# Float32 weights in place for both layers of experts 0 to 4, high and low parts in both layers of experts 5 to 7

## The chip, the cores and the metric

The kernel runs on one core of a Trainium2 chip. The metric is the device time of one execution in microseconds (us), the median of several runs. The profiles show one profiled execution each; their times are counted from the first instruction.

## The reference, cut to what matters

```python
def _moe2_ref(x, w_gate, w1, w2):            # N, D = 2304, 512; E = 8 experts; F = 1024
    N, D = x.shape
    E = w_gate.shape[1]
    cap = N // E                              # 288 tokens for each expert
    logits = x @ w_gate
    order = np.argsort(-logits.flatten())     # best (token, expert) pairs first
    ...                                       # a pair is taken if its token is free
    ...                                       # and its expert has under cap tokens
    out = np.zeros((N, D), dtype=np.float32)
    for e in range(E):
        mask = assigned == e
        h = np.maximum(x[mask] @ w1[e], 0.0)
        out[mask] = h @ w2[e]
    return out.astype(np.float32)

def reference(**kwargs):
    attn_out = _attn_ref(...)                 # 4 x 8 heads, 576 positions, causal, decayed
    x = attn_out.transpose(0, 2, 1, 3).reshape(2304, 512)
    x = _moe_ref(x=x, ...)                    # relu(x @ w_in)**2 @ w_out, 512 -> 2048 -> 512
    return _moe2_ref(x=x, ...)                # the part that the change touches
```

All inputs and the output are float32.

## The kernel before, in words

The kernel has three parts that overlap in time: attention, the first feed-forward layer (`moe1_chunk`), and the routed experts (`phase` and `expert`). The change touches only the last, which runs from about 685 us to the end.

**Routing.** `phase(m)` is called for m = 0 to 7. Each call finds the expert that fills up next, in what order is a matter of the data, and the 288 tokens that belong to it. It is one long chain of small VectorE (DVE) instructions with trips to TensorE (PE) between them: three rounds, each of which builds one-hot matrices on DVE (L1009, L1012), counts with 18 small matmuls (L1023), sums with two more (L1028, L1038), and shifts and masks on DVE (L1034, L1037, L1039, L997 and following). The last phase has no rounds. The result is the expert's number `ei` and the token list `idx`. Phase m+1 can't begin before phase m has its result. "Expert m" below is the one that phase m finds.

**Experts.** `expert(m, idx, widx)` reads the expert's number into a register of SyncE (SP), which issues the weight loads: four transfers of 512 KB for each of the two layers (for m = 0 the first layer has eight of 256 KB). GpSimd (POOL) gathers the 288 token rows by three indirect transfers (`xg`, L1151). TensorE transposes them (L1218), and the two layers follow: `up(f)` for eight blocks of 128 hidden features (L1234 to L1236, four steps k each, 32 groups in all) and, for each of four output blocks d, eight steps f (L1259, 32 in all). The result is copied (`ys`), transposed back (L1275), copied (`yo`) and written out by three indirect transfers of POOL (L1282).

**Two ways to multiply.** In *high and low parts* a matrix is split in two float32r matrices: the high part is a rounded copy (ScalarE, ACT, L381 from `rnd`), the low part is the difference (POOL, L1190; DVE may do it for m = 0 alone). A product is then three matmuls: high by high, low by high, high by low. A weight chunk lands in a raw buffer `wr` (four of them) and takes one slot for the high and one for the low part. In *plain float32* a chunk lands in its slot by the DMA itself, nothing is split, and a product is one matmul instruction, which the trace shows as two records. Before the change the first layer is in parts for all eight experts; the second is plain for m = 0 to 6 (`PLAIN = range(E - 1)`) and in parts for m = 7.

**Slots.** The weights lie in 32 slots named `z`, 16 for the first layers and 16 for the second (`us`). High parts take only the eight even ones of their 16, low parts only the odd ones; a plain chunk takes any of the 16, the even ones first.

**What sets the order.** Every operation is a task with a cost for each engine that could do it (`s.op({"pe": ...})`) and a priority (`s.base`). `Sched.run` simulates these costs once, when the kernel is built, and picks for each engine the ready task of the highest priority; `Sched.emit` writes the instructions in that order. So each engine works through a fixed list, and waits if the next instruction of its list isn't ready, whatever stands behind it. Routing has priority over the gather, and the gather over the rest of an expert (`20 + m`, `28.5 + m`, `30 + m`). The simulated costs know nothing of one engine slowing another.

Of the kernel before, what the change touches and what calls it, by code (L numbers as in the profile page):

```python
# [8 lines left out]
F = mybir.dt.float32  # L9
R = mybir.dt.float32r  # L10
# [11 lines left out]
CAP = NT // E  # L22
# [14 lines left out]
HV = [0]  # L37
# [3 lines left out]
UT = [("pt", 0), ("sc", 0), ("sc", 1)]  # L41
NH = 8

PLAIN = range(E - 1)
NX = 1
NWR = 4
YA = [("acc", 0), ("acc", 1)]
# [4 lines left out]
WG = 0  # L52
# [266 lines left out]
def dve1(n):  # L319
    return 70 + 1.04 * n  # L320
# [6 lines left out]
def act(n, psum=False, extra=0):  # L327
    return (51 if psum else 93) + 0.833 * n + 93 * extra
# [38 lines left out]
class K:  # L367
# [774 lines left out]
    def expert(self, m, idx, widx):  # L1142
        s, nc, ep = self.s, self.nc, self.ep
        IO = bass.IndirectOffsetOnAxis
        whi, wlo = [[], []], [[], []]
        plain = m in PLAIN
        xg = s.buf(ep, [96, 3, DM], F, "xg", 1)

        def gather_x():
# [11 lines left out]
        def wload(which, i):  # L1161

            src = (self.w1, self.w2)[which].rearrange("e p f -> p e f")
            us = [t for t in range(16) if (t % 4 >= 2) == which]
            if which and plain:
                wt = s.buf(self.wp, [128, 1024], F, "w1p", 0, also=[("z", 2 * t + x) for x in range(2) for t in us])
                whi[which].append(wt)

                def load(c0, c1, hold=False, after=None):
                    s.op({"sp": 450.0}, lambda e: e.dma_start(  # L1170
                        out=wt.t, in_=src[:, bass.ds(ev["v"], 1), 1024 * i:1024 * i + 1024].rearrange("p e f -> p (e f)")),
                        r=[widx] + ([(xg, WG)] if hold else []), w=[wt], nbytes=128 * 4096, after=after)
                return load
            raw = s.buf(ep, [128, 1024], F, "wr", NWR) if m else s.buf(self.wp, [128, 1024], F, "wr0", 0, also=self.zs(12, 13))
            hi = s.buf(self.wp, [128, 1024], R, f"w{which}h", 0, also=[("z", 2 * t) for t in us])
            lo = s.buf(self.wp, [128, 1024], R, f"w{which}l", 0, also=[("z", 2 * t + 1) for t in us])
            whi[which].append(hi)
            wlo[which].append(lo)
            halves = m == 0 and which in HV
            pr = P0 if m == 0 else None  # L1180

            def load(c0, c1, hold=False, after=None):
                key = c0 if halves else None
                s.op({"sp": 450.0}, lambda e: e.dma_start(
                    out=raw[:, 512 * c0:512 * c1], in_=src[:, bass.ds(ev["v"], 1), 1024 * i + 512 * c0:1024 * i + 512 * c1].rearrange("p e f -> p (e f)")),
                    r=[widx] + ([(xg, WG)] if hold else []), w=[(raw, key)], nbytes=128 * 2048 * (c1 - c0), after=after)
                for c in range(c0, c1):
                    cs = slice(512 * c, 512 * c + 512)
                    s.op(hi_alts(512, "act"), lambda e, cs=cs: self.rnd(e, hi[:, cs], raw[:, cs]), r=[(raw, key)], w=[(hi, c)], prio=pr)
                    s.op(lo_alts(512, LOE(m, which, i, 0, c)), lambda e, cs=cs: e.tensor_sub(lo[:, cs], raw[:, cs], hi[:, cs].bitcast(F)), r=[(raw, key), (hi, c)], w=[(lo, c)], prio=pr)  # L1190
            return load
# [23 lines left out]
        for k in range(4):  # L1215
            pt = s.buf(self.ps, [128, 512], F, "xt", 0, also=XT + (XA if m == 0 else []))
            for g in range(3):
                s.op({"pe": 107.0}, lambda e, k=k, g=g, pt=pt: e.transpose(pt[:, 96 * g:96 * g + 96], xg[:, g, k * 128:k * 128 + 128], self.ident[:96, :96]),  # L1218
                     r=[(xg, g), self.ident], w=[pt])
            h = s.buf(ep, [128, CAP], R, f"exh{k}", NX)  # L1220
            l = s.buf(ep, [128, CAP], R, f"exl{k}", NX)
            s.op({"act": act(CAP, True)}, lambda e, h=h, pt=pt: e.activation(h.t, pt[:, :CAP], AF.Copy), r=[pt], w=[h])
            s.op({"dve": dve1(CAP)}, lambda e, h=h, l=l, pt=pt: e.tensor_sub(l.t, pt[:, :CAP], h.t.bitcast(F)), r=[pt, h], w=[l])
            xh.append(h)
            xl.append(l)
        s.base = 30 + m

        def up(f):
            fs = slice(f * 128, f * 128 + 128)
            c = f // 4  # L1230
            u = s.buf(self.ps, [128, 512], F, "u", 2, also=UT)
            for k in range(4):
                def g(e, k=k):
                    e.matmul(u[:, :CAP], whi[0][k][:, fs], xh[k].t, start=(k == 0), stop=False)  # L1234
                    e.matmul(u[:, :CAP], wlo[0][k][:, fs], xh[k].t, start=False, stop=False)  # L1235
                    e.matmul(u[:, :CAP], whi[0][k][:, fs], xl[k].t, start=False, stop=(k == 3))  # L1236
                s.op({"pe": mm(CAP, 3)}, g, r=[(whi[0][k], c), (wlo[0][k], c), xh[k], xl[k]], w=[u])
            if plain:
                hh = s.buf(ep, [128, CAP], F, "ehh", NH)
                s.op({"act": act(CAP, True), "dve": dve1(CAP)}, lambda e: e.activation(hh.t, u[:, :CAP], AF.Relu) if e is nc.scalar else  # L1240
                     e.tensor_scalar(hh.t, u[:, :CAP], 0.0, None, op0=OP.max), r=[u], w=[hh])
                return hh, None
            hh = s.buf(ep, [128, CAP], R, "ehh", NH)
            s.op({"act": act(CAP, True)}, lambda e: e.activation(hh.t, u[:, :CAP], AF.Relu), r=[u], w=[hh])
            hl = s.buf(ep, [128, CAP], R, "ehl", NH)
            s.op({"dve": dve1(CAP)}, lambda e: e.scalar_tensor_tensor(hl.t, u[:, :CAP], 0.0, hh.t.bitcast(F), op0=OP.max, op1=OP.subtract), r=[u, hh], w=[hl])
            return hh, hl
# [3 lines left out]
        for d in range(4):  # L1251
            acc = s.buf(self.ps, [128, 512], F, "y", 0, also=YA)
            for f in range(8):
                def g(e, f=f, acc=acc, d=d):
                    hh, hl = hs[f]
                    wh = whi[1][f // 2]
                    ds = slice(512 * (f % 2) + d * 128, 512 * (f % 2) + d * 128 + 128)
                    if plain:
                        e.matmul(acc[:, :CAP], wh[:, ds], hh.t, start=(f == 0), stop=(f == 7))  # L1259
                        return  # L1260
                    wl = wlo[1][f // 2]
                    e.matmul(acc[:, :CAP], wh[:, ds], hh.t, start=(f == 0), stop=False)  # L1262
                    e.matmul(acc[:, :CAP], wl[:, ds], hh.t, start=False, stop=False)  # L1263
                    e.matmul(acc[:, :CAP], wh[:, ds], hl.t, start=False, stop=(f == 7))  # L1264
                if plain:
                    s.op({"pe": 1.89 * CAP}, g, r=[hs[f][0], whi[1][f // 2]], w=[acc])
                    continue
                s.op({"pe": mm(CAP, 3)}, g, r=[*hs[f], (whi[1][f // 2], f % 2), (wlo[1][f // 2], f % 2)], w=[acc])
            ys = s.buf(ep, [128, CAP], F, "ys", 2)
# [124 lines left out]
```

## Time and profile before

| | |
|---|---|
| median of 3 runs | 1049.22 us (1048.82 to 1049.54) |
| the profiled execution's own time | 1047.0 us |
| its span, first to last instruction | 1044.9 us |
| mean granted TensorE clock | 0.957 of full speed |
| PE busy | 951.6 us (91% of the span) |
| DVE busy | 646.0 us (62%) |
| ACT busy | 413.4 us (40%) |
| POOL busy | 359.6 us (34%) |
| splits of weights on POOL in the expert stage, in groups of 128x512 | 64 from `wr`, 81.3 us |

PE is the busiest engine over the whole span, but the share is an average. The 40 slices of the page show it at 5 to 9 tenths in the last third, where the granted clock falls below full speed several times too. The profiled execution's time is 2.1 us above its span, and 2.2 us below the median of the runs.

### The profile page before, as it was taken

Reading aid. Unit: us, or ns where it says so; the run is one execution under the profiler, and the core shown is the slowest. Engines: PE = TensorE matmul, PEld = TensorE weight load, DVE = VectorE, ACT = ScalarE, POOL = GpSimd, SP = SyncE. Lnnn points to the kernel's source line nnn. Section 1 sums busy time; section 2 is a strip of 40 time slices with the busy share of each in tenths; the row PEclk is TensorE's granted clock in tenths of the full one; section 3 lists DMA queues with packets and bytes.
Section 4 is the critical chain, followed back from the end, with each engine's and each line's share of the span. In section 5 each row is a group of like instructions: output and inputs, shape, how many; then the busy total and the mean of one; then the engine's idle time right before and its main releaser. Section 6 shows DMA issues by size and latency. Waiting matters only on the chain. (4 is left out here: it accounts for less than half of the span.)

```text
span 1044.9 us, 17749 instructions
## 1 busy us (share of the span) xinstructions
PE 951.6 (91%) x6315; PEld 775.2 (74%) x6315; DVE 646.0 (62%) x1951; ACT 413.4 (40%) x1118; POOL 359.6 (34%) x470
## 2 busy tenths in 40 slices
PE   6888899999999999999999999959789778899896
PEld 3555567887778987778988899848678667778785
DVE  6999985305553144457999834568888687842131
ACT  4755555445664455553434344212123123022210
POOL 2667745232213012223334211022561453264521
PEclk9997999999999999999999899969898899899899
DMA  6555542202222002203000000062363254172210
GB/s 207 198 189 184 181 158 82 91 1 81 80 71 90 1 30 85 70 25 112 2 21 1 21 1 22 1 204 65 121 207 122 85 194 174 32 273 67 66 46 24
DMA packets 39977, 96.25 MB, mean 92 GB/s; under 512 B 7784, under 2 KB 12040, under 8 KB 39760
## 3 DMA queue, kind: packets, MB, share of 16 engines
q1 hardware_dynamic: 36816, 85.67, 24.5%
q0 software_dynamic: 3072, 9.44, 3.0%
q8 instruction: 50, 0.82, 0.3%
q14 instruction: 39, 0.32, 0.1%
HBM read 85.48 MB, written 9.61 MB: 91 GB/s over the span
## 5 line engine op out<-in xcount | busy, mean ns | idle before, releaser
L692 PE MATMUL u<-xh,z 128*128 128x256 f32 x576 | 173.9, 302 | 0.7 <-ACT wraw L381 0.5
L694 PE MATMUL u<-xl,z 128*128 128x256 f32 x576 | 164.2, 285 | 0.5 <-POOL xl L676 0.5
L693 PE MATMUL u<-xh,z 128*128 128x256 f32 x576 | 164.1, 285 | 0.0
L1259 PE MATMUL acc<-ehh,z 128*128 128x288 f32 x448 | 132.1, 428 | 1.9 <-ACT ys L381 1.9
L692 PEld LDWEIGHTS u<-xh,z 128*128 128x128 f32 x576 | 110.9, 193 | 22.9 <-issue 11.7
L1190 POOL TENSOR_TENSOR z<-wr,z 128x512 fp32r<-128x512 f32 x64 | 81.3, 1300 | 123.2 <-ACT z L381 117.7
L693 PEld LDWEIGHTS u<-xh,z 128*128 128x128 f32 x576 | 111.2, 193 | 7.4
L697 ACT ACTIVATE r<-u 128x256 f32<-128x256 f32 x144 | 54.4, 380 | 147.3 <-PE u L694 136.4
L694 PEld LDWEIGHTS u<-xl,z 128*128 128x128 f32 x576 | 110.9, 192 | 0.8 <-POOL xl L676 0.8
L819 DVE CUSTOM_DVE_ANT_0 gjk<-wof,wgb 128x512 bf16<-128x512 f32 x128 | 102.8, 803 | 5.9 <-DMA wgb<-wgT 2.3
L718 PE MATMUL acc<-z,hl 128*128 128x512 f32 x256 | 101.1, 395 | 4.1 <-POOL hl L709 2.7
L709 POOL TENSOR_TENSOR hl<-r,hh 128x256 fp32r<-128x256 f32 x79 | 67.3, 854 | 107.5 <-ACT hh L381 89.9
L716 PE MATMUL acc<-z,hh 128*128 128x512 f32 x256 | 102.9, 402 | 1.2 <-POOL hh L383 1.2
L717 PE MATMUL acc<-z,hh 128*128 128x512 f32 x256 | 101.5, 397 | 0.0
L1259 PEld LDWEIGHTS acc<-ehh,z 128*128 128x128 f32 x448 | 81.0, 199 | 23.6 <-issue 6.9
L520 ACT ACTIVATE p<-p,st 128x576 f32<-128x576 f32 (+4 forms) x144 | 79.9, 556 | 45.9 <-DVE st L513 45.2
L513 DVE CUSTOM_DVE_ANT_0 p<-sc,row 128x192 f32<-128x192 f32 (+4 forms) x133 | 60.4, 466 | 45.2 <-PE pt L552 17.1
L1234 PE MATMUL u<-exh,z 128*128 128x288 f32 x216 | 78.5, 363 | 0.0
L508 POOL TENSOR_TENSOR row<-maskb,row 128x128 f32<-128x128 bf16 (+1 forms) x80 | 39.2, 494 | 110.6 <-DVE st L513 86.5
L496 PE MATMUL sc<-qk,qk 64*128 64x512 f32 (+5 forms) x322 | 65.2, 465 | 10.6 <-DMA qk<-in_k_dram 6.1
L1236 PE MATMUL u<-exl,z 128*128 128x288 f32 x216 | 65.3, 302 | 0.0
L1235 PE MATMUL u<-exh,z 128*128 128x288 f32 x216 | 65.3, 302 | 0.0
(346 smaller groups left out, 2030.2 us busy)
## 6 DMA issues: line engine op xcount, KB each, us to landing
wr<-in_w_dram SPq DMA_DIRECT2D x32, 512.0 KB
z<-in_w_dram SPq DMA_DIRECT2D x28, 512.0 KB
z<-in_w_in_dram SPq DMA_DIRECT2D x16, 512.0 KB
row<-cumd SPq DMA_DIRECT2D x28, 288.0 KB
z<-in_w_out_dram SPq DMA_DIRECT2D x14, 512.0 KB
vr<-in_v_dram SPq DMA_DIRECT2D x14, 320.0 KB
qk<-in_q_dram SPq DMA_DIRECT2D x15, 288.0 KB
wraw<-rd SPq DMA_DIRECT2D x32, 128.0 KB
```

The costliest lines, as they stand in the source:

```text
L520: s.op({"act": act(w, extra=2)}, lambda e, x=x, si=si, i=i, n=n, w=w, p=p[x], st=st[x]: e.activation(p[:n, :w], p[:n, :w], AF.Exp, bias=st ...
L692: e.matmul(u[:, :256], wh[:, k % 2, fs], xh[k].t, start=(k == 0), stop=False)
L693: e.matmul(u[:, :256], wl[:, k % 2, fs], xh[k].t, start=False, stop=False)
L694: e.matmul(u[:, :256], wh[:, k % 2, fs], xl[k].t, start=False, stop=(k == 3))
L709: s.op(lo_alts(256), lambda e: e.tensor_sub(hl(), r.t, hh().bitcast(F)), r=[r, kh], w=[kl])
L716: g = [lambda e, t=t, ts=ts: e.matmul(acc[t].t, hh()[:, ts], wh[:, f % 2], start=(f == 0), stop=False), lambda e, t=t, ts=ts: e.matmul(acc ...
L717: lambda e, t=t, ts=ts: e.matmul(acc[t].t, hh()[:, ts], wl[:, f % 2], start=False, stop=False),
L718: lambda e, t=t, ts=ts: e.matmul(acc[t].t, hl()[:, ts], wh[:, f % 2], start=False, stop=(f == 15))]
L819: s.op({"dve": dve1(DM) + 85}, lambda e, f=f, x=x, wo=wo, jk=jk: e.tensor_tensor_reduce(out=jk.t, in0=wo.t, in1=wb[:, x, :], scale=1.0, sc ...
L1190: s.op(lo_alts(512, LOE(m, which, i, 0, c)), lambda e, cs=cs: e.tensor_sub(lo[:, cs], raw[:, cs], hi[:, cs].bitcast(F)), r=[(raw, key), (h ...
L1234: e.matmul(u[:, :CAP], whi[0][k][:, fs], xh[k].t, start=(k == 0), stop=False)
L1259: e.matmul(acc[:, :CAP], wh[:, ds], hh.t, start=(f == 0), stop=(f == 7))
```

## The change: what it does

`PLAIN` becomes a pair, one range for each layer, and both are `range(5)`. For m = 0 to 4 the first layer is computed in plain float32 as well: its chunks land straight in their slots, the tokens are copied once (by ACT or DVE) in place of a high part by ACT and a low part by DVE, and each step of `up` is one plain matmul. For m = 5 and 6 the second layer is computed in high and low parts, as it was for m = 7 already: its chunks go through `wr`, are split by ACT and POOL, the hidden features are split by ACT (L1244) and DVE (L1246), and each step is three matmuls. The planned cost of a plain matmul is 1.69 ns a column in place of 1.89.

```diff
--- before.py
+++ after.py
@@ -41,7 +41,7 @@
 UT = [("pt", 0), ("sc", 0), ("sc", 1)]
 NH = 8
 
-PLAIN = range(E - 1)
+PLAIN = (range(5), range(5))
 NX = 1
 NWR = 4
 YA = [("acc", 0), ("acc", 1)]
@@ -1143,7 +1143,7 @@
         s, nc, ep = self.s, self.nc, self.ep
         IO = bass.IndirectOffsetOnAxis
         whi, wlo = [[], []], [[], []]
-        plain = m in PLAIN
+        plain = [m in x for x in PLAIN]
         xg = s.buf(ep, [96, 3, DM], F, "xg", 1)
 
         def gather_x():
@@ -1162,14 +1162,14 @@
 
             src = (self.w1, self.w2)[which].rearrange("e p f -> p e f")
             us = [t for t in range(16) if (t % 4 >= 2) == which]
-            if which and plain:
-                wt = s.buf(self.wp, [128, 1024], F, "w1p", 0, also=[("z", 2 * t + x) for x in range(2) for t in us])
+            if plain[which]:
+                wt = s.buf(self.wp, [128, 1024], F, f"w{which}p", 0, also=[("z", 2 * t + x) for x in range(2) for t in us])
                 whi[which].append(wt)
 
                 def load(c0, c1, hold=False, after=None):
                     s.op({"sp": 450.0}, lambda e: e.dma_start(
-                        out=wt.t, in_=src[:, bass.ds(ev["v"], 1), 1024 * i:1024 * i + 1024].rearrange("p e f -> p (e f)")),
-                        r=[widx] + ([(xg, WG)] if hold else []), w=[wt], nbytes=128 * 4096, after=after)
+                        out=wt[:, 512 * c0:512 * c1], in_=src[:, bass.ds(ev["v"], 1), 1024 * i + 512 * c0:1024 * i + 512 * c1].rearrange("p e f -> p (e f)")),
+                        r=[widx] + ([(xg, WG)] if hold else []), w=[(wt, c0 if m == 0 and which in HV else None)], nbytes=128 * 2048 * (c1 - c0), after=after)
                 return load
             raw = s.buf(ep, [128, 1024], F, "wr", NWR) if m else s.buf(self.wp, [128, 1024], F, "wr0", 0, also=self.zs(12, 13))
             hi = s.buf(self.wp, [128, 1024], R, f"w{which}h", 0, also=[("z", 2 * t) for t in us])
@@ -1217,7 +1217,11 @@
             for g in range(3):
                 s.op({"pe": 107.0}, lambda e, k=k, g=g, pt=pt: e.transpose(pt[:, 96 * g:96 * g + 96], xg[:, g, k * 128:k * 128 + 128], self.ident[:96, :96]),
                      r=[(xg, g), self.ident], w=[pt])
-            h = s.buf(ep, [128, CAP], R, f"exh{k}", NX)
+            h = s.buf(ep, [128, CAP], F if plain[0] else R, f"exh{k}", NX)
+            if plain[0]:
+                s.op({"act": act(CAP, True), "dve": dve1(CAP)}, lambda e, h=h, pt=pt: self.rnd(e, h.t, pt[:, :CAP]), r=[pt], w=[h])
+                xh.append(h)
+                continue
             l = s.buf(ep, [128, CAP], R, f"exl{k}", NX)
             s.op({"act": act(CAP, True)}, lambda e, h=h, pt=pt: e.activation(h.t, pt[:, :CAP], AF.Copy), r=[pt], w=[h])
             s.op({"dve": dve1(CAP)}, lambda e, h=h, l=l, pt=pt: e.tensor_sub(l.t, pt[:, :CAP], h.t.bitcast(F)), r=[pt, h], w=[l])
@@ -1230,12 +1234,16 @@
             c = f // 4
             u = s.buf(self.ps, [128, 512], F, "u", 2, also=UT)
             for k in range(4):
+                if plain[0]:
+                    s.op({"pe": 1.69 * CAP}, lambda e, k=k: e.matmul(u[:, :CAP], whi[0][k][:, fs], xh[k].t, start=(k == 0), stop=(k == 3)), r=[(whi[0][k], c), xh[k]], w=[u])
+                    continue
+
                 def g(e, k=k):
                     e.matmul(u[:, :CAP], whi[0][k][:, fs], xh[k].t, start=(k == 0), stop=False)
                     e.matmul(u[:, :CAP], wlo[0][k][:, fs], xh[k].t, start=False, stop=False)
                     e.matmul(u[:, :CAP], whi[0][k][:, fs], xl[k].t, start=False, stop=(k == 3))
                 s.op({"pe": mm(CAP, 3)}, g, r=[(whi[0][k], c), (wlo[0][k], c), xh[k], xl[k]], w=[u])
-            if plain:
+            if plain[1]:
                 hh = s.buf(ep, [128, CAP], F, "ehh", NH)
                 s.op({"act": act(CAP, True), "dve": dve1(CAP)}, lambda e: e.activation(hh.t, u[:, :CAP], AF.Relu) if e is nc.scalar else
                      e.tensor_scalar(hh.t, u[:, :CAP], 0.0, None, op0=OP.max), r=[u], w=[hh])
@@ -1255,15 +1263,15 @@
                     hh, hl = hs[f]
                     wh = whi[1][f // 2]
                     ds = slice(512 * (f % 2) + d * 128, 512 * (f % 2) + d * 128 + 128)
-                    if plain:
+                    if plain[1]:
                         e.matmul(acc[:, :CAP], wh[:, ds], hh.t, start=(f == 0), stop=(f == 7))
                         return
                     wl = wlo[1][f // 2]
                     e.matmul(acc[:, :CAP], wh[:, ds], hh.t, start=(f == 0), stop=False)
                     e.matmul(acc[:, :CAP], wl[:, ds], hh.t, start=False, stop=False)
                     e.matmul(acc[:, :CAP], wh[:, ds], hl.t, start=False, stop=(f == 7))
-                if plain:
-                    s.op({"pe": 1.89 * CAP}, g, r=[hs[f][0], whi[1][f // 2]], w=[acc])
+                if plain[1]:
+                    s.op({"pe": 1.69 * CAP}, g, r=[hs[f][0], whi[1][f // 2]], w=[acc])
                     continue
                 s.op({"pe": mm(CAP, 3)}, g, r=[*hs[f], (whi[1][f // 2], f % 2), (wlo[1][f // 2], f % 2)], w=[acc])
             ys = s.buf(ep, [128, CAP], F, "ys", 2)
```

## Rows read from the trace of the kernel before

**Rows 1.** The page's first part, share of the span and instructions of TensorE.
```profile
PE 951.6 (91%) x6315; PEld 775.2 (74%) x6315; DVE 646.0 (62%) x1951; ACT 413.4 (40%) x1118; POOL 359.6 (34%) x470
```

**Rows 2.** Windows by routing period: length, busy PE, PEld, DVE, ACT, POOL; clock, DMA.
```profile
724.85:762.72 37.87, 31.24 (x215) 25.72 (x214) 32.09 (x108) 7.93 (x18) 18.00 (x17) 0.91 0.42 143
762.72:799.55 36.83, 30.23 (x211) 25.34 (x210) 31.17 (x104) 9.82 (x22) 14.71 (x11) 0.91 0.39 131
799.55:836.51 36.96, 30.45 (x232) 26.80 (x231) 27.04 (x105) 9.15 (x21) 16.22 (x17) 0.91 0.42 146
836.51:874.72 38.21, 30.05 (x235) 26.64 (x233) 29.11 (x103) 9.99 (x22) 17.20 (x17) 0.96 0.42 142
874.72:912.29 37.57, 30.87 (x210) 25.19 (x208) 31.63 (x107) 6.59 (x14) 13.79 (x11) 0.91 0.36 128
912.29:1034.00 121.71, 117.29 (x738) 104.08 (x737) 36.44 (x105) 23.50 (x51) 48.00 (x55) 0.97 0.30 99
```

**Rows 3.** Timeline of TensorE: where it stood idle longest, start, length, [idle before <-releaser].
```profile
747.22 0.48 PE L1023 MATMUL ov<-ph_G,ph_OH 128*128 128x128 bf16 x3 [3.54 <-DVE ph_G L1012]
...
785.19 0.80 PE L1023 MATMUL ov<-ph_G,ph_OH 128*128 128x128 bf16 x6 [5.84 <-DVE ph_G L1012]
...
817.39 0.17 PE L1038 MATMUL ov<-ph_PB,rc_ones 128*128 128x8 bf16 x1 [5.03 <-DVE ph_PB L1037]
...
855.15 0.17 PE L1038 MATMUL ov<-ph_PB,rc_ones 128*128 128x8 bf16 x1 [4.83 <-DVE ph_PB L1037]
...
897.82 0.80 PE L1023 MATMUL ov<-ph_G,ph_OH 128*128 128x128 bf16 x6 [4.18 <-DVE ph_G L1012]
```

**Rows 4.** Timeline of VectorE and GpSimd ahead of those idle times.
```profile
739.45 6.16 POOL L1190 TENSOR_TENSOR z<-wr,z 128x512 fp32r<-128x512 f32 x5
739.68 5.97 DVE L997 TENSOR_SCALAR ph_ti<-ph_P,ph_th 128x18 int32<-128x18 f32 x1
...
775.79 7.82 DVE L997 TENSOR_SCALAR ph_ti<-ph_P,ph_th 128x18 int32<-128x18 f32 x1
...
814.05 3.29 DVE L1037 TENSOR_SCALAR ph_PB<-rc_blk,ph_cnt 128x8 bf16<-128x8 f32 x1
...
849.51 5.59 DVE L1037 TENSOR_SCALAR ph_PB<-rc_blk,ph_cnt 128x8 bf16<-128x8 f32 x1
...
889.92 6.32 DVE L997 TENSOR_SCALAR ph_ti<-ph_P,ph_th 128x18 int32<-128x18 f32 x1
```

**Rows 5.** One line's instructions: L997 on VectorE, duration ns min/median/max.
```profile
L997 DVE TENSOR_SCALAR ph_ti<-ph_P,ph_th x12: 227/236/7823, 704.2 to 904.6; 128x18 int32<-128x18 f32 x12
```

**Rows 6.** Groups by line on GpSimd: the splits of weights, total and mean of one.
```profile
L1190 POOL TENSOR_TENSOR z<-wr,z 128x512 fp32r<-128x512 f32 x64 | 81.3, 1300 | 123.2 <-ACT z L381 117.7 <-ACT ehh L1240 5.3
```

**Rows 7.** Timeline of ScalarE and TensorE: waits behind splits on ScalarE.
```profile
732.61 0.63 ACT L381 ACTIVATE z<-wr 128x512 fp32r<-128x512 f32 x1 [1.29 <-DMA wr<-in_w_dram]
...
733.60 0.75 PE L1259 MATMUL acc<-ehh,z 128*128 128x288 f32 x2 [1.89 <-ACT ys L381]
...
846.75 0.53 PE L1275 MATMUL sc<-ident,ys 128*96 128x128 f32 x3 [2.50 <-ACT ys L381]
```

**Rows 8.** Timeline at the start of expert 0.
```profile
701.87 0.42 PE L1218 MATMUL pt<-ident,xg 96*128 96x96 f32 x1 [6.04 <-DMA xg<-x2d,ph_idx]
...
706.37 1.55 DVE L1009 TENSOR_TENSOR ph_OH<-rc_i,ph_q 128x768 bf16<-128x768 bf16 x1
```

**Rows 9.** The chain that ended last, in order of time: steps of either product.
```profile
982.32 0.13 PE u L1234
...
983.11 0.48 PE acc L1259 x2
...
996.40 5.82 PE acc L1259 x24
```

**Rows 10.** The same chain and TensorE's timeline, at the gather for expert 7.
```profile
966.44 5.45 DMA xg<-x2d,ph_idx
...
971.94 0.42 PE L1218 MATMUL pt<-ident,xg 96*128 96x96 f32 x1 [3.08 <-DMA xg<-x2d,ph_idx]
```

## The prediction

> **What bounds the kernel now.** I read the page's engine shares first, then the windows of the expert stage cut at the moments at which SP issues the weights of a new expert (that is where a routing phase ends), then the idle time of PE inside them, and then what DVE and POOL did just before. The page says PE, 91% of the span [rows 1]. The windows show that this is two regimes [rows 2]. From 912 us to the end PE is busy 117.3 of 121.7 us: there its work is the bound. In the five periods before, each of 37 to 38 us, it is busy only some 30 to 31, and in four of the five the clock is granted at 0.91 on the mean, between the levels of 2.4 and 1.2 GHz. There something else sets the pace. TensorE's own timeline names it: once in each period PE stands still for 3.5 to 5.8 us for a routing instruction whose input DVE hasn't made [rows 3]. And DVE isn't slow because it has much to do: at these places one instruction over 18 or 8 columns takes 3.3 to 7.8 us [rows 4], where the median of that line is 236 ns [rows 5]. In the first case shown, POOL began a run of five weight splits 0.2 us earlier, and DVE's instruction ended when POOL's run did (739.45 + 6.16 = 745.61; 739.68 + 5.97 = 745.65) [rows 4]. So the reader is to see this chain: POOL splits, DVE is held, routing is late, PE waits at the next routing matmul of its fixed list, the clock falls after the wait. The splits are those of the first layer's weights, 8 per expert for m = 1 to 7 and 8 for m = 7's second layer, 64 in all [rows 6].
>
> **The change part by part.** All terms start from the profiled execution's 1047.0 us.
>
> *First layer plain, m = 1 to 4: no splits in four periods.* This removes 32 splits of POOL (1.30 us each [rows 6], 41.6 us) and 32 copies by ACT. POOL's own time is worth nothing by itself; what counts is the wait on PE. The four waits are 3.54 + 5.84 + 5.03 + 4.83 = 19.2 us [rows 3]. They end when DVE ends, so I take them off whole. What is late next is DVE's own chain; that has its own term below. **-19.2.**
>
> *The clock after these waits.* At 0.91, 0.91, 0.91 and 0.96 the four periods lose 0.09 x 37.87 + 0.09 x 36.83 + 0.09 x 36.96 + 0.04 x 38.21 = 11.6 us of full speed [rows 2]. The clock fell after each of the long waits, and PE had work at hand, so with the waits these go. Bounds: 0, if smaller waits still bring the clock down, to 11.6. **-11.6.**
>
> *ACT's queue.* Two more waits of PE, 1.89 and 2.50 us, are for a copy `ys` on ACT; ahead of the first of them ACT's list held a split that waited for its weights to land (idle 1.29 us for DMA) [rows 7]. For m = 1 to 4 no such split is left. **-4.4.**
>
> *Expert 0.* Its first layer lands in place too; before, POOL split 5 of 8 pieces and DVE 3, and DVE instructions of routing that run beside these splits are stretched (the first of three takes 1.55 us [rows 8]). But the long wait at this place, 6.04 us, is for the gathered tokens [rows 8], whose transfer stands behind 4 MB of weights, and these stay. Bounds 0 and 5; nearer the middle, since some of the routing ahead of the gather gets shorter. **-2.5.**
>
> *The matmuls themselves.* Two triples of parts take 983.11 - 982.32 = 0.79 us, 0.395 each; a plain one takes 0.48, twelve in a row 5.82, so 0.485 [rows 9]. A layer has 32 steps, so plain costs 32 x 0.09 = 2.88 us more. Five first layers become plain, two second layers cease to be: (5 - 2) x 2.88. PE's list is fixed and its work must be done sometime, so I count all of it as on the path, though in a period with a wait left over some would lie beside it. **+8.6.**
>
> *DVE's chain against PE's list.* With the waits gone, who sets a period? A period less the long hold leaves 32.1, 29.2, 33.9 and 32.9 us for the chain (hold = length in [rows 4] less 0.24); less PE's wait, the ACT wait and the lost clock it leaves 29.0, 27.7, 28.6 and 29.4 us of PE work. So the chain could still be longer by 3.1 + 1.5 + 5.3 + 3.5 = 13.4 us. But it also carries shorter holds at the start of each run of splits, and four low parts of the tokens on DVE, which both go. Bounds 0 and 13.4; I take a quarter, nearer the lower end. The copy of the tokens that remains, on ACT or DVE, is one where there were two. **+3.5.**
>
> *Second layer in parts, m = 5 and 6.* This adds 16 splits on POOL (16 x 1.30 = 20.8 us), 16 copies on ACT, and 16 low parts of hidden features on DVE. After 912 us DVE is busy 36 of 122 us, ACT 23.5, POOL 48 [rows 2]; so DVE's and ACT's parts are hidden, and POOL has the room but not necessarily at the right time. Expert 5's eight new splits can fall into the period after its weights are issued, where DVE is held already and PE waits 4.18 us [rows 3]: a second hold there costs up to such a wait and a clock loss, 5 + 3.4 us, or nothing if full even slots push them past the last round. Expert 6's stand ahead of the gather for expert 7, which PE waits for already [rows 10]. The eight more weight transfers pass through the four raw buffers, so SP holds the later experts' loads behind them. Bounds 0 and 20.8 plus three clock losses of 3.4, 31; I take 5 in the period and 2 at the gather, since the planned order has room. **+7.0.**
>
> *The planned cost* (544 to 487 ns for 288 columns) and the halves in which expert 0's loads are issued change the order alone: 0, within the bounds above.
>
> Sum: 1047.0 - 19.2 - 11.6 - 4.4 - 2.5 + 8.6 + 3.5 + 7.0 = 1028.4 us. The median of the runs stands 2.2 us above the profiled execution, so about **1031 us** as it is measured.
>
> **A rule weighed.** In this trace DVE's instruction is held over a run of five splits, 5.97 us [rows 4], and POOL did not let it in between two of them. The Trainium skill (SBUF — State Buffer, "Who interferes with whom") says that the port pair that VectorE shares with GpSimd is an exclusive lock, held by whichever comes first for its whole instruction. By that, a hold would last at most one split. Had the rule the last word, the long holds would mostly have another cause, and the first two terms would be wrong. The row decides for the forecast, and the rule's case is the fourth rival.
>
> **The rivals.**
>
> *PE is never held at all* (rival 1). With less in routing's way, the short holds and low parts gone too, the chain keeps ahead of PE, and expert 5's splits come after the last round. Then +3.5 and +7.0 go, and so do the wait of 4.18 us and the 3.4 us of clock in the fifth period: 1030.6 - 10.5 - 7.6 = 1012 us. For it: DVE is busy 32 of 38 us only with the holds in. Against: the chain's length without them is above PE's in every period.
>
> *The chain takes the place of the hold* (rival 2). The whole 13.4 us of difference stays (9.9 more than counted), and two clock losses of 3.4 with it: 1030.6 + 9.9 + 6.8 = 1047 us. For it: 33.9 against 28.6 us in the third period. Against: the short holds are part of these numbers.
>
> *POOL's list becomes the bound of the end, slower* (rival 3). POOL works in order, so a split that waits for a slot holds the gather behind it. If all 16 new splits end up as PE time and three waits bring the clock down, 31 us stand in place of 7: 1030.6 + 24 = 1055 us. It decides from a cost of 28 us on (over 1051). For it: the gather for expert 7 lies on the chain that ended last already [rows 10]. Against: 48 of 122 us busy, with 21 to come.
>
> *The holds are not POOL's doing* (rival 4). Then the removed splits save at most one length of a split at each of four places, 5.2 us in place of 19.2 + 11.6, and 1030.6 + 25.6 = 1056 us. This is what the rule weighed above would give. Against: five long DVE instructions, and the one shown beside POOL ends with its run.
>
> **How the numbers follow.** Chances: forecast 0.53 (its own range 1020 to 1041), rival 1 0.20, rival 2 0.09, rival 3 0.12, rival 4 0.06. A measurement can tell about 0.2% from no change, that is 1047.1 to 1051.3 us. Faster: 0.52 + 0.20 + 0.05 = 0.77. Same: 0.01 + 0.04 + 0.02 + 0.01 = 0.08. Slower: 0.10 + 0.05 = 0.15. The range 1007 to 1050 leaves out about 0.05 of rival 1 below and 0.15 of rivals 3 and 4 above.
>
> **What would show it.** In the profile after: no POOL split between the first issue of expert 1's weights and that of expert 5's; L997 and L1037 at their short length there; routing periods of some 29 to 31 us; no PE wait over 3 us at L1023 or L1038 in them, and a clock of 1.0. First-layer steps of 0.48 us for m = 0 to 4, second-layer triples of 0.39 for m = 5 and 6. The last stretch longer than 122 us, since routing ends earlier with more PE work left. The prediction is wrong if PE waits as long for other routing instructions, or if long DVE instructions remain without POOL beside them, or if PE stands idle more than 15 us at gathers near the end.

## The result, and the profile after

The changed kernel takes 1019.45 us (median of 4 runs, 1017.74 to 1022.8) against 1049.02 us for the kernel before (4 runs): the ratio is 0.9726, 95% interval 0.9698 to 0.9755. The forecast was 1031 us; the gain is 29.6 us where 18 were forecast. The profiled execution took 1019.41 us, with a span of 1017.6 us.

The page's first part, to be read beside [rows 1]: busy time, share of the span, instructions.

```profile
PE 943.7 (93%) x6219; PEld 761.7 (75%) x6219; DVE 616.1 (61%) x1940; ACT 402.6 (40%) x1098; POOL 331.7 (33%) x449
```

PE's share rose from 91% to 93%, which says little. The windows of the kernel after say where it rose, cut at the same events as [rows 2], with the first period ahead of them (length, busy PE, PEld, DVE, ACT, POOL; clock, DMA):

```profile
683.51:724.01 40.50, 28.11 (x163) 21.42 (x162) 21.23 (x103) 2.97 (x7) 4.85 (x3) 0.75 0.40 125
724.01:753.13 29.12, 29.01 (x197) 23.19 (x197) 21.97 (x103) 3.79 (x9) 7.41 (x9) 1.00 0.55 185
753.13:783.57 30.44, 30.44 (x202) 24.22 (x201) 23.69 (x109) 2.38 (x6) 3.95 (x4) 1.00 0.45 159
783.57:813.07 29.50, 29.50 (x197) 23.52 (x196) 21.28 (x102) 4.89 (x12) 7.17 (x8) 1.00 0.53 184
813.07:843.12 30.05, 29.44 (x193) 23.32 (x192) 21.21 (x102) 3.43 (x8) 7.54 (x9) 1.00 0.52 179
843.12:891.38 48.26, 33.11 (x199) 25.88 (x198) 40.75 (x105) 12.55 (x25) 24.02 (x19) 0.82 0.31 100
891.38:1007.00 115.62, 112.56 (x789) 105.02 (x788) 36.35 (x104) 34.13 (x77) 57.56 (x63) 0.99 0.33 104
```

The second to fifth lines are the four periods that lost their splits: 119.11 us in sum where it was 149.87, PE busy in 118.4 of them, the clock at 1.00. The sixth is the fifth period, and it went the other way, from 37.57 to 48.26 us. What PE waited for in those four periods, over 724 to 843 us, and the two lines of routing that were long before:

```profile
PE ov L1028 <- DVE ph_h L385: 0.6, 1, 0.6
...
L997 DVE TENSOR_SCALAR ph_ti<-ph_P,ph_th x14: 235/236/16702, 668.2 to 882.6; 128x18 int32<-128x18 f32 x14
...
L1037 DVE TENSOR_SCALAR ph_PB<-rc_blk,ph_cnt x21: 218/231/232, 667.3 to 889.0; 128x8 bf16<-128x8 f32 x21
```

One wait of 0.6 us is all that stands where [rows 3] had four of 3.5 to 5.8. L1037 is short everywhere. L997 is long once, 16.70 us, and that is the fifth period. VectorE's and GpSimd's timelines there, and TensorE's where it waited longest for routing, and for the gathers of experts 0, 6 and 7:

```profile
857.29 17.16 POOL L1190 TENSOR_TENSOR z<-wr,z 128x512 fp32r<-128x512 f32 x14
...
857.79 16.70 DVE L997 TENSOR_SCALAR ph_ti<-ph_P,ph_th 128x18 int32<-128x18 f32 x1
...
876.07 2.14 PE L1023 MATMUL ov<-ph_G,ph_OH 128*128 128x128 bf16 x13 [14.43 <-DVE ph_G L1012]
...
699.28 0.42 PE L1218 MATMUL pt<-ident,xg 96*128 96x96 f32 x1 [6.88 <-DMA xg<-x2d,ph_idx]
...
919.19 0.40 PE L1218 MATMUL pt<-ident,xg 96*128 96x96 f32 x1 [2.09 <-DMA xg<-x2d,ph_idx]
...
954.66 0.30 PE L1218 MATMUL pt<-ident,xg 96*128 96x96 f32 x1 [0.88 <-DMA xg<-x2d,ph_idx]
```

POOL's run of 14 splits ends at 857.29 + 17.16 = 874.45 us, DVE's instruction at 857.79 + 16.70 = 874.49, and PE stands still for 14.43 us. (L1012, which PE waits for, stands behind L997 in DVE's list.) It is the pattern of [rows 4] with 14 splits in place of five: expert 5, now in parts in both layers, has 16 splits, and the fixed lists put 14 of them into one run.

**Where the time went.** I cut both profiled executions into windows of 1 us, took busy PE times the granted clock as work, busy PE times what the clock lacked as clock loss, and the rest as idle (us, after less before; good to some 0.5):

| stretch | length | idle | clock loss | work |
|---|---|---|---|---|
| start of the stage | -1.6 | | | |
| first period | +0.8 | -0.7 | 0.0 | +1.6 |
| four periods, m = 1 to 4 | -30.8 | -27.2 | -8.9 | +5.3 |
| fifth period | +10.7 | +8.5 | +0.2 | +2.1 |
| from there to the end | -6.4 | -1.7 | -1.4 | -3.1 |

The lengths add up to -27.3 us, the difference of the spans (1017.6 - 1044.9). The stage begins 1.6 us earlier, ahead of anything that the change touches; why, I don't know.

### The profile page after: what moved, and what is told of

It reads as the page before. It is cut to its first block, busy times and chain, and to the rows that moved or that the text cites. A ratio compares the mean times of both kernels' runs of the same rounds, so it can differ in the third digit from the quotient of the medians.

```text
span 1017.6 us, 17471 instructions
## 1 busy us (share of the span) xinstructions
PE 943.7 (93%) x6219; PEld 761.7 (75%) x6219; DVE 616.1 (61%) x1940; ACT 402.6 (40%) x1098; POOL 331.7 (33%) x449
## 5 line engine op out<-in xcount | busy, mean ns | idle before, releaser
L1267 PE MATMUL acc<-ehh,z 128*128 128x288 f32 x320 | 91.4, 422 | 0.0
L1238 PE MATMUL u<-exh,z 128*128 128x288 f32 x280 | 82.6, 424 | 0.1
L1190 POOL TENSOR_TENSOR z<-wr,z 128x512 fp32r<-128x512 f32 x48 | 59.6, 1274 | 55.4 <-ACT z L381 55.3
L1151 POOL DMA_INDIRECT xg<-x2d,ph_idx x24 | 30.1, 1252 | 127.7 <-DVE ph_G L1012 58.9
L1267 PEld LDWEIGHTS acc<-ehh,z 128*128 128x128 f32 x320 | 58.1, 196 | 13.8 <-issue 0.5
L718 PEld LDWEIGHTS acc<-z,hl 128*128 128x128 f32 x256 | 48.2, 188 | 19.1 <-POOL hl L709 5.2
```

Source lines behind the costliest of these rows:

```text
L718: lambda e, t=t, ts=ts: e.matmul(acc[t].t, hl()[:, ts], wh[:, f % 2], start=False, stop=(f == 15))]
L1238: s.op({"pe": 1.69 * CAP}, lambda e, k=k: e.matmul(u[:, :CAP], whi[0][k][:, fs], xh[k].t, start=(k == 0), stop=(k == 3)), r=[(whi[0][k], c ...
```

## The experiments

The theory: POOL's splits hold DVE's short routing instructions, PE waits for them, and the removal of splits in four periods is the gain; the arithmetic itself costs PE time. The main rival: the gain comes from the plain layers, the landing in place or the new order, and the holds have another cause.

**Each half alone.** `first_only` keeps the second layer as it was before (plain for m = 0 to 6); `second_only` keeps the first layer as it was before (in parts for all).

```diff
-PLAIN = (range(5), range(5))
+PLAIN = (range(5), range(7))     # first_only
+PLAIN = (range(0), range(5))     # second_only
```

> The first half of the change alone: first layer plain for m = 0 to 4, second layer plain for m = 0 to 6 as before. Theory (POOL's runs of splits hold DVE's routing): the four periods after expert 1's weights stay at 29 to 31 us. In the fifth only expert 5's 8 first-layer splits are left, so its PE wait falls from 14.4 us to some 4 to 6, and two plain second layers cost 2 x 2.9 more: 1019.5 - 9.5 + 5.8 = about 1016 us (1011 to 1021). Rival (the second half of the change, less PE work near the end, carries a good part of the gain): 1035 or more.

Measured: 1014.73 us (1008.13 to 1016.86), ratio 0.9667 (0.9617 to 0.9718). The first half alone brings the whole gain. Its fifth period, POOL, DVE and PE:

```profile
858.43 7.37 POOL L1190 TENSOR_TENSOR z<-wr,z 128x512 fp32r<-128x512 f32 x6
...
858.93 6.92 DVE L997 TENSOR_SCALAR ph_ti<-ph_P,ph_th 128x18 int32<-128x18 f32 x1
...
867.42 1.74 PE L1023 MATMUL ov<-ph_G,ph_OH 128*128 128x128 bf16 x12 [4.35 <-DVE ph_G L1012]
```

Six splits and a hold of 6.92 us, where the whole change has 14 and 16.70. So the eight added splits of expert 5 cost PE 14.43 - 4.35 = 10.1 us of waiting.

> The second half of the change alone: first layer in parts for all eight, second layer in parts for m = 5 to 7. Theory: the four periods are as they were before the change (37 us, PE waits of 3.5 to 5.8 us, long DVE instructions beside POOL's splits), the fifth gets expert 5's 16 splits and grows by some 10 us, and two second layers cost 5.8 less: 1049 + 10 - 5.8 = about 1053 us (1045 to 1058). Rival (less PE work near the end carries it): under 1044.

Measured: 1039.89 us (1035.9 to 1046.62, 10 runs), ratio 0.9932 (0.9906 to 0.9958): a miss, as I expected no gain. PE's waits from 720 to 915 us and the longest hold:

```profile
PE ov L1038 <- DVE ph_PB L1037: 20.8, 3, 9.0
PE ov L1023 <- DVE ph_G L1012: 13.5, 5, 6.6
...
L1037 DVE TENSOR_SCALAR ph_PB<-rc_blk,ph_cnt x21: 223/231/9672, 669.9 to 925.3; 128x8 bf16<-128x8 f32 x21
```

The four periods have their holds still, the longest of each 7.21, 6.29, 9.62 and 8.11 us, and the fifth's grew to 9.67 us (6.32 in [rows 4]). The time is in the range that I had given the rival (under 1044 us, from less PE work near the end), but it is only a quarter of the change's gain. Two plain layers fewer are 2 x 2.88 = 5.8 us less PE work by [rows 9], near the 7.4 us gained; that this is the reason is argued, not shown. The profiled execution (1046.62) is the slowest of the ten runs, and where the others save their 7 us this trace can't say.

**POOL's work put back, nothing else.** `dummy_pool` is the kernel after, and for m = 1 to 4 POOL subtracts each first-layer chunk from itself into a raw buffer that nobody reads: 32 extra subtractions of the size of a split. They take 1.04 us each by the median, where a split takes 1.30 [rows 6].

```diff
+                    if which == 0 and 1 <= m <= 4:
+                        scr = s.buf(ep, [128, 1024], F, "wr", NWR)
+                        for c in range(c0, c1):
+                            cs = slice(512 * c, 512 * c + 512)
+                            s.op({"pool": ptt(512)}, lambda e, cs=cs: e.tensor_sub(scr[:, cs], wt[:, cs], wt[:, cs]), r=[wt], w=[scr])
```

> The kernel after, and for m = 1 to 4 POOL also computes, for each half chunk of the first layer's weights that has landed, a 128x512 difference of it with itself into a raw buffer that nobody reads: the 32 POOL instructions that the change took away are back, and nothing else (no ACT copy, no landing in raw buffers, no products in parts). Theory: DVE instructions of 4 to 8 us and PE waits of 3 to 6 us are back in the four periods, which grow from 30 to some 37 us: 1019.5 + 30 = about 1050 us (1038 to 1056). Rival (the gain came from weights that land in place, from ACT's shorter list or from the other products; POOL beside DVE costs nothing): within 1023.

Measured: 1047.38 us (1045.14 to 1052.98), ratio 1.0006 (0.9986 to 1.0026). All of the gain is gone. Its four periods, PE's waits over them (us in total, times, longest), and the first hold:

```profile
725.30:762.00 36.70, 32.55 (x198) 26.04 (x198) 29.81 (x107) 3.85 (x9) 15.48 (x17) 0.91 0.43 148
762.00:797.50 35.50, 31.90 (x197) 25.16 (x196) 29.76 (x105) 2.13 (x5) 12.37 (x11) 0.95 0.39 135
797.50:835.30 37.80, 32.49 (x202) 25.65 (x199) 29.67 (x103) 5.03 (x12) 14.73 (x17) 0.91 0.42 143
835.30:872.00 36.70, 33.76 (x200) 26.26 (x198) 27.88 (x104) 3.58 (x9) 15.65 (x17) 0.91 0.42 147
...
PE ov L1023 <- DVE ph_G L1012: 15.3, 12, 5.0
...
739.34 5.02 POOL L1177 TENSOR_TENSOR wr<-z 128x512 f32<-128x512 f32 x5
...
739.26 5.14 DVE L997 TENSOR_SCALAR ph_ti<-ph_P,ph_th 128x18 int32<-128x18 f32 x1
...
745.98 0.51 PE L1023 MATMUL ov<-ph_G,ph_OH 128*128 128x128 bf16 x6 [2.75 <-DVE ph_G L1012]
```

146.7 us in place of 119.1: 15.3 more of idle, 10.4 of clock loss, 2.0 of work. The windows are cut to within 0.7 us, so some 27 of the 30.8 us that the change gained in these periods are lost again. The plain layers, the landing in place and ACT's short queue are all still there; POOL is busy again, and DVE's 18-column instruction lasts as long as POOL's run of five and ends with it. Reading the chunks also keeps their slots longer and the planned order is a new one, but PE waits over these periods for DVE's `ph_G` alone, for no transfer and not for ACT. This is the theory's main proof.

**The splits moved, the arithmetic untouched.** `before_dve` and `before_dve_all` are the kernel *before*, with the low parts made by DVE itself, for m = 1 to 4 or for all m.

```diff
-LOE = lambda m,w,i,j,c: "dve pool" if m==0 else "pool"
+LOE = lambda m,w,i,j,c: "dve pool" if m==0 else "dve" if m<5 else "pool"     # before_dve
+LOE = lambda m,w,i,j,c: "dve"                                                # before_dve_all
```

> The kernel before, with the first layers' low parts of m = 1 to 4 on DVE in place of POOL; everything stays in parts. DVE, the busier engine, gets 8 x 0.68 = 5.4 us more work in each of four periods. Theory: the holds go all the same, with them the PE waits of 3.5 to 5.8 us and the low clock; DVE's own work takes back a part: 1047 - 31 + 4 x 3 = about 1028 us (1018 to 1038). Rival (what counts is how much DVE and POOL have to do, not that POOL's runs hold DVE): 1047 or more.

Measured: 1015.8 us (1013.95 to 1018.92), ratio 0.9706 (0.9679 to 0.9734), better than I expected: 32 splits more on DVE cost less than I gave them. A stretch over its four periods, and L997:

```profile
728.00:849.00 121.00, 116.00 (x906) 100.29 (x905) 103.11 (x437) 42.30 (x96) 31.71 (x30) 1.00 0.52 173
...
L997 DVE TENSOR_SCALAR ph_ti<-ph_P,ph_th x14: 227/236/238, 670.5 to 877.6; 128x18 int32<-128x18 f32 x14
```

DVE is busy 103 of 121 us, and still PE waits for 5.0 us only: DVE's 32 splits of 0.68 us cost PE far less than POOL's 32 did.

> The kernel before, with every low part of weights on DVE: no plain first layer at all, and none of POOL's splits. Against the run with m = 1 to 4 on DVE (1015.8 us), theory: the PE wait of 6.3 us in the fifth period with its clock loss of 3.4, the 1.6 in the last phase and a part of the gather's 2.8 go: 1015.8 - 12 = about 1004 us (998 to 1010). That would be the gain of the whole change and more without any of its arithmetic.

Measured: 1003.45 us (1002.56 to 1005.76), ratio 0.9601 (0.9569 to 0.9633), the fastest median of all kernels here, 16 us below the change (13 by the ratios, each against the kernel before on its own chip). A stretch of its expert stage, and the group of its splits (total, mean ns):

```profile
725.00:880.00 155.00, 150.11 (x1161) 129.97 (x1160) 134.57 (x571) 50.62 (x114) 37.63 (x39) 1.00 0.52 175
...
L1190 DVE TENSOR_TENSOR z<-wr,z 128x512 fp32r<-128x512 f32 x64 | 41.5, 684 | 9.6 <-ACT z L381 9.4
```

A split takes DVE 0.68 us where POOL took 1.30 [rows 6].

**The fifth period.** If expert 5's splits beside its routing are what made it longer, it must shrink when expert 5 has none (`six`, `seven`), grow back with eight (`six_five`), shrink when DVE makes them (`dve5`), and perhaps when POOL leaves gaps between them (`spaced`).

```diff
-PLAIN = (range(5), range(5))
+PLAIN = (range(6), range(6))     # six
+PLAIN = (range(7), range(7))     # seven
+PLAIN = (range(6), range(5))     # six_five
```

> Both layers plain for m = 0 to 5, parts for 6 and 7. Theory: no split is left in a period with rounds, so the fifth period falls from 47.5 us to 30 and its PE wait of 14.4 us and the clock after it go; one more expert in plain costs 2 x 2.9: 1019.5 - 14.4 - 4.5 + 5.8 = about 1006 us (1002 to 1011). Rival (the end is bound by PE's work alone and the wait in the fifth period is covered by work later): 1019.5 + 5.8 = 1025.

Measured: 1009.15 us (1007.36 to 1013.4), ratio 0.9648 (0.9607 to 0.9689), within what was expected. L997 over the whole of `six`, then POOL, DVE and PE in the last phase, beside expert 6's splits:

```profile
L997 DVE TENSOR_SCALAR ph_ti<-ph_P,ph_th x14: 235/236/238, 667.1 to 861.5; 128x18 int32<-128x18 f32 x14
...
874.48 7.45 POOL L1190 TENSOR_TENSOR z<-wr,z 128x512 fp32r<-128x512 f32 x6 [22.12 <-ACT z L381]
...
875.89 1.15 DVE L1091 TENSOR_TENSOR ph_scn<-ph_scn,ph_M 128x36 f32<-128x36 f32 x1
877.08 1.18 DVE L1093 TENSOR_TENSOR ph_P<-ph_scn 128x18 f32<-128x18 f32 x1
878.30 1.19 DVE L1095 TENSOR_SCALAR ph_gm<-ph_P 128x18 f32<-128x18 f32 x1
...
882.80 1.60 PE L1119 MATMUL ov<-ph_gi,ph_OH 128*96 128x6 bf16 x18 [3.80 <-DVE ph_OH L1105]
```

No hold is left in the periods with rounds, and `six` gains on the change with 5.8 us more PE work (two more plain layers). In the last phase a hold of another kind is left: beside POOL's run of six splits five DVE instructions take 1.15 to 1.30 us each, about a split's length, where the same lines took 0.17 to 0.27 us at their turn before (871 to 872.7 us), and PE waits for 3.80 us. Here DVE got in between the splits.

> Both layers plain for m = 0 to 6, parts for m = 7 alone. No split stands beside any routing at all. Against the kernel with six plain experts the PE wait of 3.8 us in the last phase, the low clock after it (3.4) and the wait for a gather (1.5) can go, and 5.8 us of PE work come on top: 1009 - 8.7 + 5.8 = about 1006 us (1004 to 1014). If those waits are covered: 1015.

Measured: 1009.26 us (1008.19 to 1012.11), ratio 0.9641 (0.9615 to 0.9667). It is level with `six`, though two more plain layers add 5.8 us of PE work; the wait of 3.80 us in the last phase is gone from its trace, which makes up for a part of that.

> First layer plain for m = 0 to 5, second layer plain for m = 0 to 4, the rest in parts: against the kernel with six plain experts expert 5's second layer goes back to parts, with 8 splits and 2.9 us less PE work. If its splits fall beside the rounds of the fifth period, a hold of some 7 us, a PE wait of 4 to 5 and a clock loss of 3.4 come back: 1009 - 2.9 + 8 = about 1014 us. If they come after the rounds: 1006. The theory puts them beside the rounds (its weights are issued at the start of that period): 1014 (1009 to 1018).

Measured: 1018.02 us (1015.07 to 1020.04), ratio 0.9708 (0.9683 to 0.9733), at the upper end of what was expected. Its longest hold, and PE's wait for it:

```profile
L1037 DVE TENSOR_SCALAR ph_PB<-rc_blk,ph_cnt x21: 218/231/7386, 668.9 to 881.3; 128x8 bf16<-128x8 f32 x21
...
864.54 0.17 PE L1038 MATMUL ov<-ph_PB,rc_ones 128*128 128x8 bf16 x1 [6.53 <-DVE ph_PB L1037]
```

The eight splits of a second layer alone bring back a hold of 7.39 us, on another instruction, and 6 us of time by the ratios (9 by the medians).

```diff
-LOE = lambda m,w,i,j,c: "dve pool" if m==0 else "pool"
+LOE = lambda m,w,i,j,c: "dve" if m==5 else "pool"     # dve5
```

> The kernel after, with expert 5's 16 low parts on DVE in place of POOL (DVE took 0.68 us for one in the trace before). Theory (it is POOL's run of instructions that holds DVE, not the work of splitting): no DVE instruction over 2 us is left in the fifth period, the PE wait of 14.4 us and the clock after it go, and DVE's 10.9 us lie partly beside its waits for PE: 1019.5 - 19 + 4 = about 1004 us (999 to 1011). Rival (the splits have to be done and take their time from the routing chain on either engine): 1014 to 1020.

Measured: 1006.45 us (1005.36 to 1008.3), ratio 0.9609 (0.9586 to 0.9632). DVE's timeline in the fifth period:

```profile
852.90 2.48 DVE L1190 TENSOR_TENSOR z<-wr,z 128x512 fp32r<-128x512 f32 x4
...
858.49 0.23 DVE L997 TENSOR_SCALAR ph_ti<-ph_P,ph_th 128x18 int32<-128x18 f32 x1
```

With the same arithmetic and the same number of splits as the change, 12 us go by the ratios (13 by the medians), by moving 16 of them. L997 takes 0.23 us.

In `spaced` POOL sets one element of a scrap buffer after each of expert 5's splits.

```diff
-... lambda e, cs=cs: e.tensor_sub(lo[:, cs], raw[:, cs], hi[:, cs].bitcast(F)), ...
+... lambda e, cs=cs: (e.tensor_sub(lo[:, cs], raw[:, cs], hi[:, cs].bitcast(F)), e.memset(self.spacer.t, 0.0) if m == 5 else None), ...
```

> The kernel after, and behind each of expert 5's 16 splits POOL clears one element (0.09 us each). Theory A (DVE is held for as long as POOL's splits follow each other without anything between): the long DVE instruction of 16.7 us falls to under 3, DVE gets in once between two splits, and the PE wait falls from 14.4 us to 6 to 12: 1008 to 1017. Theory B (POOL keeps DVE out over short instructions as well): the DVE instruction stays at 16 to 19 us, 1019.5 + 1.5 = 1021 us.

Measured: 1020.92 us (1017.34 to 1021.1), ratio 0.9752 (0.9718 to 0.9787), no better than the change. POOL, DVE and PE in the fifth period:

```profile
858.32 1.28 POOL L1190 TENSOR_TENSOR z<-wr,z 128x512 fp32r<-128x512 f32 x1
859.53 0.09 POOL L1190 MEMSET spacer<- 1x1 f32 x1
859.58 1.27 POOL L1190 TENSOR_TENSOR z<-wr,z 128x512 fp32r<-128x512 f32 x1
...
858.81 17.11 DVE L997 TENSOR_SCALAR ph_ti<-ph_P,ph_th 128x18 int32<-128x18 f32 x1
...
877.49 0.80 PE L1023 MATMUL ov<-ph_G,ph_OH 128*128 128x128 bf16 x6 [14.84 <-DVE ph_G L1012]
```

DVE was held over splits and memsets alike. What would let it in stays open, but the traces divide the cases. In all of them the runs of splits that held DVE until their end stand straight behind POOL's indirect transfers (in the kernel after, the last gather ends at 857.27 us and the run of 14 begins at 857.29). Beside runs that POOL began after waiting for ACT, as in `six` and at the start of the periods before the change, DVE's instructions took 1.2 to 1.7 us, a split at a time. No run tests whether the transfers ahead are the reason.

**All splits on DVE, with the change.** `after_dve` is the kernel after with `LOE` always "dve"; `parts_dve` is that with `PLAIN = (range(0), range(5))`.

> The kernel after, with every low part of weights (m = 5, 6, 7) on DVE, none on POOL. Against the kernel with expert 5's alone on DVE (1006.5 us), theory: the PE wait of 3.3 us in the last phase and the low clock after it (3.4) go, and gathers no longer stand behind splits: 1006.5 - 7 = about 1000 us (996 to 1005). Rival (that wait is covered by later work): 1006.

Measured: 1010.63 us (1009.71 to 1013.67), ratio 0.9661 (0.9632 to 0.9691): a miss, slower than `dve5`. POOL's gathers for an expert near the end, and PE's wait for the last of them:

```profile
904.07 1.17 POOL L1151 DMA_INDIRECT xg<-x2d,ph_idx  x1 [5.20 <-PE acc L1267]
905.54 1.85 POOL L1151 DMA_INDIRECT xg<-x2d,ph_idx  x1 [0.30 <-DVE z L1190]
907.70 0.92 POOL L1151 DMA_INDIRECT xg<-x2d,ph_idx  x1 [0.30 <-issue]
...
912.67 0.42 PE L1218 MATMUL pt<-ident,xg 96*128 96x96 f32 x1 [4.14 <-DMA xg<-x2d,ph_idx]
```

PE's wait in the last phase (3.3 us in `dve5`) is gone, as expected, but its waits for gathers come to 7.5 us where `dve5` has 2.0. POOL's second gather takes 1.85 us where the third takes 0.92, and DVE is at its splits. That the hold runs in the other direction there is argued, and it would explain about 1 us only; what causes the rest of the miss is open.

> First layer in parts for all eight, second layer plain for m = 0 to 4 and in parts for 5 to 7, every low part of weights on DVE: 5 x 2.9 us less PE work than the kernel after with all on DVE, but 5.4 us more for DVE in each routing period. Theory (with the holds gone PE's work is the bound, and DVE has room): 1000 - 14 + 4 periods x 2 = about 994 us (988 to 1002). Rival (DVE's chain becomes the bound of the periods): 1003 or more.

Measured: 1005.02 us (1002.03 to 1005.68), ratio 0.9613 (0.9583 to 0.9642), 3 us above the expected range, where I had placed the rival that DVE's chain bounds the periods (1003 or more), and level with `before_dve_all` and `dve5` within the intervals. The rival is not the reason: over the first four periods PE is busy 123.77 of 124.95 us. POOL in the fifth period, and PE's wait:

```profile
857.10 1.05 POOL L1151 DMA_INDIRECT xg<-x2d,ph_idx  x1 [28.55 <-DVE ph_base L974]
...
858.46 3.51 POOL L1290 DMA_INDIRECT out_dram<-yo,ph_idx  x1 [0.22 <-ACT ehh L1248]
...
865.97 0.94 POOL L1151 DMA_INDIRECT xg<-x2d,ph_idx  x1 [0.31 <-issue]
...
871.84 0.42 PE L1218 MATMUL pt<-ident,xg 96*128 96x96 f32 x1 [7.61 <-DMA xg<-x2d,ph_idx]
```

The second gather is issued 8.9 us after the first. POOL's list has three transfers of results between them, and these took 3.51, 1.87 and 1.22 us, where such a transfer takes 0.92 to 0.95 us late in the kernel after. So some 5 us are the planned order and some 4 a stretch of POOL's own work, with DVE busy beside it. Whether DVE is the cause of the stretch no run tests.

## Why the prediction was right, and where its terms were off

The measured 1019.45 us is 11.6 us below the forecast, just under the forecast's own range (1020 to 1041) and nearer to rival 1's 1012; the stretches below say why.

**The mechanism** held: POOL's splits hold DVE, DVE's delay stops PE, the clock falls after it. `dummy_pool` brings the loss back with POOL alone, and `before_dve` and `before_dve_all` take it away with no arithmetic changed. The fourth rival is out.

**The four waits, ACT's queue, the clock (-19.2, -4.4, -11.6: -35.2 in sum)** measured -27.9 for all idle time of the four periods before and -8.9 for the clock, -36.8 in sum. It came out near because two errors went against each other. The idle time was 4.3 us more than the waits that I had listed, in waits of which none was over 1.1 us. The clock gave 2.7 us less: I had multiplied a period's mean clock by its whole length, and part of the low clock fell in the time in which PE stood idle. No run changes ACT's queue alone, so its 4.4 us are not shown by themselves.

**DVE's chain against PE's list (+3.5)** measured +0.7, the idle time that the four periods kept. So nearly all of the 13.4 us by which the chain seemed longer was not the chain's own. Most of it must be holds as well, the short ones: `before_dve`, which keeps the low parts of the tokens and adds DVE 32 splits, takes 121 us for the four periods, where the chain without the long holds had come out at 128. Rival 2 is out, and in these periods rival 1 was the nearer one.

**The matmuls (+8.6)** measured +5.9 over the whole stage by the table's method (work 277.8 to 283.7 us), +5.3 of it in the four periods, where 11.5 were counted. Why a plain layer costs less than 2.88 us there, I don't know.

**The second layer in parts (+5 in the fifth period, +2 at the gather)** measured +8.7 of idle time and lost clock in the fifth period (the rest of its 10.7 us is work) and -3.1 from there to the end. In sum that is +5.6 where +7.0 was forecast, near by luck: the two halves are off by 3.7 and 5.1 us, against each other. For the fifth period I had priced one more hold of the size of those in [rows 4] and hoped that full slots would push some splits back; instead 14 splits went into one run and the hold was as long as the run. `first_only` against the whole change (4.35 and 14.43 us of waiting), `six_five` and `dve5` show it from three sides. At the end POOL had the room: the wait for the gather of expert 7 fell from 3.08 [rows 10] to 0.88 us, that for expert 6's rose from 1.18 to 2.09. So the third rival is out, though POOL's list did cost PE 10.1 us of waiting, elsewhere than at the end. One sign came out the other way for the same reason: the last stretch was to be longer than 122 us and is 115.6, since the fifth period was the longer one.

**Expert 0 (-2.5)** measured -0.7 of idle time (the period is 0.8 us longer, with 1.6 more of work in it). The wait for the gather, 6.04 us before [rows 8], is 6.88 now, behind the same transfers, so what DVE saved ahead of it bought little.

These terms add up to -25.3 us; with the 1.6 us by which the stage begins earlier it is -26.9, and the spans differ by 27.3.

**The rule weighed.** DVE's instruction was held over 14 splits, 16.70 us, and over 14 pairs of split and memset, 17.11 us. The Trainium skill (SBUF — State Buffer, "Who interferes with whom") has the shared port pair held for a whole instruction by whoever issues first, where VectorE's instruction uses that pair too; whether L997's form does, no run shows by itself. The trace agrees that one engine blocks the other fully, as DVE's end falls on POOL's within 0.04 us. The bound that I drew from it, one split at most, doesn't hold there; it fits in the last phase of `six`, where each stretched instruction takes 1.15 to 1.30 us.

By stretches, forecast against measured in the profiled execution: to the end of the first period +0.4 (-2.5 and a plain layer's 2.88) against -0.8; the four periods -20.2 (-35.2 + 3.5 + 4 x 2.88) against -30.8; the fifth +5.0 against +10.7; the rest -3.8 (+2.0 and two plain layers fewer) against -6.4. In sum -18.6 against -27.3: the four periods gave 10.6 us more than forecast, and the fifth took 5.7 of them back.

## What to carry to other kernels

Look in the trace for a short VectorE instruction that lasts as long as a run of GpSimd's: busy shares count it as work, and it is a wait. Such a hold can be as long as the whole run beside it, so a change that lengthens the run can lengthen the hold; in other places here each instruction was held for one split, so read in the trace which of the two it is. Giving GpSimd's work to the "busier" VectorE can win: here that alone, one line of the kernel before, gave 4.0% where the change gave 2.7%.

## What the runs showed of the hardware that was not expected

- A VectorE `tensor_scalar` of 18 columns, 0.236 us by its median, took 16.70 us beside 14 `tensor_tensor` of GpSimd back to back, and 17.11 us with memsets of 0.09 us between them. Beside another run of six splits (`six`) five such short instructions took 1.15 to 1.30 us each.
- The subtraction of a split, 128x512 in float32, takes 0.68 us on VectorE and 1.25 to 1.30 us on GpSimd.
- The mean granted clock of a stretch overstates what it costs: the fifth period after shows 0.82 over 48.26 us, which would be 8.7 us, but PE's busy time lost 2.7, since much of the low clock lay in its idle time.
